# Computing only one token of each mirrored pair directly, and storing the output from compact columns in merged pieces

## The chip, the cores and the metric

The kernel runs on one core of a Trainium2 chip. The metric is the device time of one execution, in microseconds (us). Each kernel was run several times, beside runs of the kernel before on the same chip.

## The reference

The input x has 8 batches of 3008 tokens of 256 elements. The reference takes the real part of a two-dimensional Fourier transform of each batch and feeds every token through a gated feed-forward layer:

```python
X = np.fft.fft(np.fft.fft(x, axis=1), axis=2).real        # 8 x 3008 x 256
t = X.reshape(24064, 256)
out = (np.maximum(t @ w_gate, 0) * (t @ w_val)) @ w_out   # 256 -> 1536 -> 256, float32
```

The input is real, so token r and token 3008 − r of a batch have the same cosine part and sine parts of opposite sign. The kernel uses this: it computes the gate and the value of a "direct" token with two matmuls each, gets the gate of its "mirrored" token with one more matmul, and the mirrored value in most steps on VectorE. A mirrored token is therefore the cheaper one.

## The kernel before

A batch is 3008 = 94 × 32 tokens. The kernel takes it in three blocks of 512 direct columns, each in 12 steps (`f`, one per 128 hidden units), 288 steps in all. The 512 columns are four groups `g` of four quarters of 32. 1536 direct and 1472 mirrored columns make up the 3008 tokens, and each row is stored once. But for 31 pairs both tokens are among the direct ones, although one of them could be had by mirroring.

```python
def mirrored(t):                      # columns whose mirrored token is computed too
    blk = steps[t][1]
    return slice(NB if blk == 0 else 0, 512 - NB if blk == NBLK - 1 else 512)      # NB = 32

def gate(t):                          # value(t, part) has the same form, with wc[1], ws[1]
    ...
    nc.tensor.matmul(e["G"][:], lhsT=wc[0][:, fs], rhs=pq[:, 0, :], start=True, stop=False)
    nc.tensor.matmul(e["G"][:], lhsT=ws[0][:, fs], rhs=pq[:, 1, :], start=False, stop=True)
    nc.scalar.activation(e["gs"][:], e["G"][:], ACTF.Relu)
    # [cut: memset of the 32 columns of h that have no mirrored token]

def out_piece(t, half):               # output matmuls: 128 tokens x 256, summed over 12 f
    ...                               # into po, copied to os (128 x 4 x 256), then:
            if s == 3:
                store(b, blk, sg, os_)

def store(b, blk, sg, os_):           # four transfers of 32 partitions, up to 4 KB a partition
    for u in range(4):
        ka = NKA * u + 4 * blk
        src = os_[32 * u:32 * u + 32].rearrange("p g d -> p (g d)")
        if sg == 0:
            nc.sync.dma_start(out=view(out, (b * S + ka) * D, [[NA * D, NB], [1, 4 * D]]), in_=src)
            continue
        # [cut: the mirrored side, the same with 3 or 4 groups]
```

The next batches are prepared while one is computed. Of the following work the DMAs (all but a small indexed load of POOL's) go through the same queue, SP's, as the stores:

```python
# per batch: load x of batch b+2, fold it on POOL, transform batch b+1 (stage1),
# pass it through DRAM (shuffle_out, shuffle_in), rotate (one matmul), stage2
#     load step, fold step, stage1 steps, shuffle step, rotate step, stage2 steps
plan = {0: (18, 24, (18, 19, 20, 21, 22, 23, 24, 25), 26, 32, (33, 34, 35, 37, 39, 41)),
        1: (7, 13, range(6, 14), 14, 22, (23, 25, 27, 29, 31, 33)),
        2: (7, 13, range(4, 20, 2), 20, 26, (27, 28, 30, 32, 34, 36))}      # batches 2 to 7
op = ctx.enter_context(tc.tile_pool(name="op", bufs=2, space=SB))           # the os tiles
ep = ctx.enter_context(tc.tile_pool(name="ep", bufs=4, space=SB))           # gm, E
```

## Time and profile before

| | before |
|---|---|
| device time, median of 3 runs | 650.03 us (649.75 to 650.68) |
| span of the profiled run | 648.3 us |
| mean granted TensorE clock | 0.987 |

From the page of the kernel before: the span, busy time of each engine (share, instructions), the granted clock in 40 slices in tenths, all DMA packets, the chain that ended last by engine, and the stores.

```profile
span 648.3 us, 12804 instructions
PE 626.1 (97%) x4170; PEld 408.8 (63%) x4246; DVE 565.0 (87%) x889; ACT 425.1 (66%) x813; POOL 508.1 (78%) x716
PEclk9699999999999999999999999999999999999999
DMA packets 32823, 70.77 MB, mean 109 GB/s; under 512 B 4650, under 2 KB 22146, under 8 KB 30754
PE 89%; DVE 6%; issue 2%; DMA 2%; ACT 1%; SPq 0%; DVEq 0%; ACTq 0%
out_dram<-os SPq DMA_DIRECT2D x173, 128.0 KB
```

TensorE bounds this kernel: it is busy 97% of the span and is 89% of the chain. The clock is at 90% or more from the third slice on. A window of one whole batch says the same. Its columns are start:end and length, then busy time and instructions of PE, PEld, DVE, ACT and POOL, the granted clock, the DMA share and GB/s.

```profile
390.00:464.00 74.00, 73.37 (x506) 49.27 (x515) 68.17 (x107) 51.03 (x98) 64.88 (x94) 1.00 0.45 113
```

The timeline of PE around the rotate matmul of the same batch (start, duration, line, what; a bracket at the end would tell idle time before it) has no gap. The rotate, L194, starts 0.22 us after a 512-column matmul.

```profile
390.68 0.38 PE L497 MATMUL V<-pq,ws 128*128 128x512 bf16 x1
390.90 0.18 PE L194 MATMUL psr<-t,rot 128*128 128x12 bf16 x1
390.93 0.60 PE L546 MATMUL po<-wo,h 128*128 128x256 bf16 x4
```

The list of waits (engine, line, what it waited for: total us, times, longest) has nothing at the rotate, and only small entries for what feeds PE. (POOL waits for x in two halves, `xl` and `xh`; the list has 9.3 us more for `xh`.)

```profile
ACT gm L488 <- POOL h L511: 3.4, 6, 0.6
PE G L485 <- ACT gs L475: 2.2, 2, 1.1
POOL eo L99 <- DMA xl<-in_x_dram: 2.2, 1, 2.2
PE po L546 <- DVE os L551: 1.1, 2, 0.6
```

### The profile page before, as it was taken

Reading aid. Unit: us, or ns where it says so; the run is one execution under the profiler, and the core shown is the slowest. Engines: PE = TensorE matmul, PEld = TensorE weight load, DVE = VectorE, ACT = ScalarE, POOL = GpSimd, SP = SyncE. Lnnn points to the kernel's source line nnn. Section 1 sums busy time; section 2 is a strip of 40 time slices with the busy share of each in tenths; the row PEclk is TensorE's granted clock in tenths of the full one; section 3 lists DMA queues with packets and bytes.
Section 4 is the critical chain, followed back from the end, with each engine's and each line's share of the span. In section 5 each row is a group of like instructions: output and inputs, shape, how many; then the busy total and the mean of one; then the engine's idle time right before and its main releaser. Section 6 shows DMA issues by size and latency. Waiting matters only on the chain.

```text
span 648.3 us, 12804 instructions
## 1 busy us (share of the span) xinstructions
PE 626.1 (97%) x4170; PEld 408.8 (63%) x4246; DVE 565.0 (87%) x889; ACT 425.1 (66%) x813; POOL 508.1 (78%) x716
## 2 busy tenths in 40 slices
PE   7888999999999999999999999999999999999995
PEld 3424666666666666666666666666666666666664
DVE  8857688889898998989989998989988988989991
ACT  5465676776766667677676666676666766766660
POOL 9648669967998799968998699967998666666660
PEclk9699999999999999999999999999999999999999
DMA  9792483295125551195334752285312142112113
GB/s 234 241 234 46 104 215 85 69 208 168 40 82 120 143 161 45 47 199 146 81 74 115 165 148 55 50 177 152 96 50 73 31 131 73 50 34 64 32 41 88
DMA packets 32823, 70.77 MB, mean 109 GB/s; under 512 B 4650, under 2 KB 22146, under 8 KB 30754
## 3 DMA queue, kind: packets, MB, share of 16 engines
q1 hardware_dynamic: 30228, 58.03, 33.9%
q0 software_dynamic: 2336, 11.80, 8.7%
q8 instruction: 33, 0.54, 0.4%
q14 instruction: 34, 0.28, 0.1%
q10 hardware_dynamic: 192, 0.13, 0.1%
HBM read 39.77 MB, written 30.96 MB: 109 GB/s over the span
## 4 chain that ended last, share of the span: by engine, by line
PE 89%; DVE 6%; issue 2%; DMA 2%; ACT 1%; SPq 0%; DVEq 0%; ACTq 0%
PE po L546 38%; PE V L497 10%; PE G L474 9%; PE G L485 9%; PE V L495 8%; PE G L473 8%; PE ps L164 2%; PE ps L206 2%; DVE E L505 2%; DVE h L499 1%; PE V L523 1%; PE psw L263 1%; DMA xl<-in_x_dram 1%; DVE eo L136 1%; DVE eo L132 1%
## 5 line engine op out<-in xcount | busy, mean ns | idle before, releaser
L511 POOL TENSOR_TENSOR h<-gm,E 128x480 bf16<-128x480 f32 (+1 forms) x251 | 307.7, 1226 | 90.9 <-DVE E L519 63.9
L546 PE MATMUL po<-wo,h 128*128 128x256 bf16 x2304 | 337.1, 272 | 2.8 <-DVE os L551 1.1
L546 PEld LDWEIGHTS <-h 128*128 128x128 bf16 x2304 | 222.7, 98 | 91.1 <-issue 3.4
L488 ACT ACTIVATE gm<-G 128x480 f32<-128x480 f32 (+1 forms) x288 | 167.4, 581 | 126.8 <-PE G L485 118.7
L499 DVE TENSOR_TENSOR h<-gs,V 128x512 bf16<-128x512 f32 x288 | 195.7, 687 | 17.6 <-ACT gm L488 11.5
L505 DVE SCALAR_TENSOR_TENSOR E<-nb,af,V 128x480 f32<-128x480 bf16 (+1 forms) x245 | 177.6, 725 | 23.3 <-PE V L495 12.6
L475 ACT ACTIVATE gs<-G 128x512 f32<-128x512 f32 x288 | 171.8, 597 | 0.8 <-PE G L474 0.8
L519 DVE SCALAR_TENSOR_TENSOR E<-E,V 128x480 f32<-128x480 f32 (+1 forms) x245 | 161.2, 658 | 0.0
L497 PE MATMUL V<-pq,ws 128*128 128x512 bf16 x287 | 108.7, 379 | 2.2 <-DVE E L505 1.7
L485 PE MATMUL G<-pq,wm 128*128 128x480 bf16 (+1 forms) x288 | 106.7, 370 | 2.2 <-ACT gs L475 2.2
L474 PE MATMUL G<-pq,ws 128*128 128x512 bf16 x281 | 106.5, 379 | 2.2 <-DVE pq L211 0.4
L495 PE MATMUL V<-pq,wc 128*128 128x512 bf16 x255 | 96.6, 379 | 0.0
L473 PE MATMUL G<-pq,wc 128*128 128x512 bf16 x253 | 95.9, 379 | 0.1
L555 ACT COPY os<-po 128x512 f32<-128x512 f32 x94 | 55.0, 585 | 60.2 <-PE po L546 60.2
L104 POOL TENSOR_TENSOR eo<-xl 94x254 bf16<-94x254 f32 (+2 forms) x100 | 74.6, 750 | 0.4
L101 POOL TENSOR_TENSOR xl<-xl,xh 94x510 f32<-94x510 f32 (+2 forms) x50 | 65.9, 1319 | 3.9
L497 PEld LDWEIGHTS <-ws 128*128 128x128 bf16 x288 | 28.2, 98 | 33.7
L474 PEld LDWEIGHTS <-ws 128*128 128x128 bf16 x288 | 28.2, 98 | 31.5 <-issue 0.2
L511 DVE TENSOR_TENSOR h<-gm,V 128x480 bf16<-128x480 f32 (+1 forms) x37 | 24.6, 665 | 22.7 <-ACT gm L488 17.1
L174 ACT CAST t<-ps 96x512 bf16<-96x512 f32 x63 | 36.9, 586 | 5.7 <-PE ps L162 5.2
L495 PEld LDWEIGHTS <-wc 128*128 128x128 bf16 x288 | 28.1, 98 | 11.0 <-issue 4.3
L485 PEld LDWEIGHTS <-wm 128*128 128x128 bf16 x288 | 28.2, 98 | 7.6 <-issue 4.1
(108 smaller groups left out, 348.1 us busy)
## 6 DMA issues: line engine op xcount, KB each, us to landing
out_dram<-os SPq DMA_DIRECT2D x173, 128.0 KB
xl<-in_x_dram SPq DMA_DIRECT2D x7, 1360.0 KB
Td<-t SPq DMA_DIRECT2D x7, 768.0 KB
t<-Td SPq DMA_DIRECT2D x7, 768.0 KB
nb<-Nd SPq DMA_DIRECT2D x24, 128.0 KB
xl<-in_x_dram SPq DMA_DIRECT2D x7, 238.0 KB
xl<-in_x_dram SPq DMA_DIRECT2D x4, 384.0 KB
xh<-in_x_dram SPq DMA_DIRECT2D x4, 384.0 KB
```

Source lines behind the costliest of these rows:

```text
L473: nc.tensor.matmul(e["G"][:], lhsT=wc[0][:, fs], rhs=pq[:, 0, :], start=True, stop=False)
L474: nc.tensor.matmul(e["G"][:], lhsT=ws[0][:, fs], rhs=pq[:, 1, :], start=False, stop=True)
L475: nc.scalar.activation(e["gs"][:], e["G"][:], ACTF.Relu)
L485: nc.tensor.matmul(e["G"][:, cols], lhsT=wm[0][:, f * 128:(f + 1) * 128], rhs=pqt[b, blk][:, 1, cols], start=False, stop=True, skip_group_ ...
L488: nc.scalar.activation(e["gm"][:, cols], e["G"][:, cols], ACTF.Relu)
L495: nc.tensor.matmul(e["V"][:], lhsT=wc[1][:, fs], rhs=pq[:, 0, :], start=True, stop=split(t))
L497: nc.tensor.matmul(e["V"][:], lhsT=ws[1][:, fs], rhs=pq[:, 1, :], start=False, stop=True, skip_group_check=split(t))
L499: nc.vector.tensor_tensor(e["h"][:, 0, :], e["gs"][:], e["V"][:], op=ALU.mult)
L505: nc.vector.scalar_tensor_tensor(e["E"][:, cols], nbt[b, blk][:, cols], af[:, f:f + 1], e["V"][:, cols], op0=ALU.mult, op1=ALU.add)
L511: eng.tensor_tensor(free(e["h"][:], 512 + cols.start + NB - 1, [NB, (cols.stop - cols.start) // NB], [-1, NB]), e["gm"][:, cols].rearrange ...
L519: nc.vector.scalar_tensor_tensor(e["E"][:, cols], e["E"][:, cols], 2.0, e["V"][:, cols], op0=ALU.mult, op1=ALU.subtract)
L546: nc.tensor.matmul(po[:, s % 2, :], lhsT=ht[t - f + ff]["h"][:, sg, g * 128:(g + 1) * 128], rhs=wo[:, ff, :], start=(ff == 0), stop=(ff == ...
```

## The change

The change stops computing both tokens of those 31 pairs directly (1505 direct columns per batch and `f` instead of 1536, and 1504 mirrored instead of 1472), drops the memsets, writes the mirrored product reversed as a whole (one flat pattern), and covers the 128 partitions of an output tile with merged transfers where it can. Columns are compact now, so a tile's rows begin in the middle of a quarter: `store` cuts the tile into pieces of equal stride and merges equal pieces.

```diff
+    LO, HI = NB // 2, 512 - NB // 2
     def mirrored(t):
-        return slice(NB if blk == 0 else 0, 512 - NB if blk == NBLK - 1 else 512)
+        return slice(LO if blk == 0 else 0, HI if blk == NBLK - 1 else 512)
+    def direct(t):
+        return slice(LO - 1 if blk == 0 else 0, HI if blk == NBLK - 1 else 512)
 ...  # gate and value on the columns of direct(t); no memset of h
-        eng.tensor_tensor(free(e["h"][:], 512 + cols.start + NB - 1, [NB, ...], [-1, NB]), ...)
+        eng.tensor_tensor(free(e["h"][:], 512 + n - 1, [-1, n]), e["gm"][:, cols], val[:, cols], op=ALU.mult)
 ...  # out_piece: the last group of a tile may have 112 or 113 tokens; its ACT copy is split in two
+            if last:                                  # the very last tile, group by group
+                nc.vector.tensor_copy(os_[0:m, g:g + 1, :], po[0:m, 0:1, :])
+                store(b, blk, sg, os_, g, g + 1, (nc.sync, nc.scalar) if g == 3 else (nc.sync,))
-        for u in range(4): ...                        # four stores of 32 partitions
+        # parts: (partition, partitions np_, group, groups ng, row), then
+        while k < len(parts):
+            w = 1
+            while ...next part has the same shape, at a constant step...: w += 1
+            queues[n % len(queues)].dma_start(
+                out=view(out, ra * D, [[step * D, w], [NA * D, np_], [1, ng * D]]),
+                in_=os_[p:p + w * np_, ga:ga + ng, :].rearrange("p g d -> p (g d)"))
```

Pieces that result: in block 0, 17, 3x32 and 15 partitions (direct), 3x32, 1, 15, 1, 15 (mirrored); in block 1, 15, 17, 3x32; in block 2, 15, 17, 2x32, 16, 16. "3x32" is one transfer from 96 partitions to three stretches of 32 rows.

## The prediction

> **What bounds it now.** TensorE: PE is busy 97% of the span and 89% of the chain that ended last (the page). By the windows view one batch takes 74.0 us, PE busy 73.4; the timeline shows a 512-column matmul every 0.215 us and an output matmul every 0.109 us, back to back, weight loads hidden. In the list of waits PE waits about 12 us in all. DVE (87%) and POOL (78%) have slack.
>
> **What the change saves.** Each of the 96 (batch, f) pairs loses 31 columns in four direct matmuls and gains 32 in the mirrored gate (and in the mirrored value for 37 unsplit steps): about 8,400 columns net, at 0.215 us per 512 3.5 us of PE, all on the critical path. POOL loses 192 memsets of 123 ns and gains about 33 ns on 167 mirrored products; ACT gets 32 more copies: off the path. Weight loads of 112 or 113 columns should cost nothing: pairs with 96 columns already start 113 ns apart.
>
> **What it adds: badly spread stores.** The built program has 294 rows on the SP queue instead of 159: the 32-partition stores become pieces of 17, 3x32, 15, 1 rows. The Trainium skill ("DMA: Bandwidth & Descriptors", "Why a DMA increments its semaphore by 16 and not by 1") says that the number k of DMA engines is the largest up to 16 that divides the slowest dimension of both sides, and that HWDGE uses the lowest-numbered k. This trace agrees where it can: the 14-partition load shows one early increment, then 14 landings; the one-row Nd store an early one, then one. So 32 rows used 16 engines, but 17 rows use 1, and 3x32 against 96 partitions 3. Engine 0 gets about 50 packets of 4 KB per output tile instead of 8. At 159 ns each (the trace's uncontended packets) a tile keeps it busy 8 us of 12.4; landing goes from 2 us to about 10.
>
> **Is that on the path?** Behind those stores, on the same ring, queue the x load and the shuffle through DRAM. Before: shuffle out 4.4 us, in 4.8, landing 4 us before the rotate matmul. Estimate with an x load: engine 0 gets a store (8.3 us), then loads until about 21 us after the start, then two more stores (16 us); the shuffle lands about 9 us late, and in-order PE waits about 5 us at the rotate matmul. Batches 2 to 5: 5 us each; batch 1 4.6, batch 0 2.5, batch 6 under 1: 28 us. Stalls may drop the granted clock: 3 us. The x fold comes 3 us later on POOL, absorbed by four E buffers. The end gets 14 SP issues of 0.43 us instead of 11: +1.5 us.
>
> **Sum.** 650 - 3.5 + 28 + 3 + 1.5 = 679 us; 80% range 650 to 712. Faster by over 2%: 0.03; within 2%: 0.22; slower by over 2%: 0.75.
>
> **What would show it.** PE busy falls about 3 us while the span grows; the waits gain "PE psr (or its weight load) <- DMA of the shuffle" once per batch, 2 to 8 us; 17-row stores show one late increment, 3x32 stores three; PEclk dips. Wrong if 3x32 stores land on 16 engines or within 3 us, or if no PE gap appears at the rotate.
>
> **What would make it wrong.** Stores split over more engines: then about 649 us. An engine slower than 159 ns a packet, or stores also blocking ACT's output copies (two os buffers): over 700.

## More of the kernel before

The waits of the SP queue show how long the second half of the shuffle waits for the first to land in DRAM: 32.5 us in 8 times, about 4 us each.

```profile
SPq L188 <- DMA Td<-t: 32.5, 8, 7.9
```

At the end, DVE copies the last output tile as soon as PE gives it:

```profile
637.44 0.42 DVE L551 COPY os<-po 128x256 f32<-128x256 f32 x1 [5.28 <-PE po L546]
...
642.72 0.42 DVE L551 COPY os<-po 128x256 f32<-128x256 f32 x1 [1.56 <-PE po L546]
```

## The result, and the profile after

| | before | after |
|---|---|---|
| device time, median | 650.16 us | 716.52 us (711.98 to 716.68, 4 runs) |
| span of the profiled run | 648.3 us | 714.8 us |
| mean granted clock | 0.987 | 0.958 |

The times of before in this table are those of the rounds of after. The change made the kernel slower: ratio 1.1003, 95% interval 1.0959 to 1.1047. A ratio here is the mean time of one kernel's runs over that of the kernel before in the same rounds, so it is not quite the ratio of the medians quoted. Executions over 1.5% slower than the fastest of the same kernel are left out of the means. The output is correct. The same lines of the page after:

```profile
span 714.8 us, 12709 instructions
PE 642.7 (90%) x4215; PEld 421.5 (59%) x4246; DVE 565.3 (79%) x889; ACT 428.8 (60%) x844; POOL 503.2 (70%) x525
PEclk8799999999999999999899998999999999999985
DMA packets 31260, 70.76 MB, mean 99 GB/s; under 512 B 3072, under 2 KB 20584, under 8 KB 29192
PE 52%; DMA 30%; DVE 5%; POOL 3%; ACT 3%; issue 2%; SPq 2%; POOLq 0%; DVEq 0%; ACTq 0%
out_dram<-os SPq DMA_DIRECT2D x32, 384.0 KB
out_dram<-os SPq DMA_DIRECT2D x39, 68.0 KB
```

PE has fewer columns to do, yet its busy time rose by 16.6 us: a lower clock makes the same matmuls longer. The DMA moved the same bytes at a lower mean rate; its share of the chain rose from 2% to 30%. The packets under 512 B fell by about 1,600: if each transfer ends with one small packet per DMA engine that it uses, the change should have 1,578 fewer. By the rule for the number of engines that the prediction names, the 203 stores of before use 16 engines each, 3,248 in all, and the 206 of after 1,670. The difference is 1,578, and the two pages differ by just that (4,650 and 3,072).

The timeline of PE after, at the same rotate. It now starts 6.22 us late, and the matmuls after it start 0.41 us apart until 432, when the 0.21 us of before comes back.

```profile
421.29 0.37 PE L503 MATMUL V<-pq,ws 128*128 128x496 bf16 x1
427.89 0.18 PE L194 MATMUL psr<-t,rot 128*128 128x12 bf16 x1 [6.22 <-DMA t<-Td]
427.91 1.02 PE L554 MATMUL po<-wo,h 128*128 128x256 bf16 x4
...
430.40 0.62 PE L483 MATMUL G<-pq,wc 128*128 128x496 bf16 x1
430.81 0.62 PE L484 MATMUL G<-pq,ws 128*128 128x496 bf16 x1
...
433.58 0.37 PE L490 MATMUL G<-pq,wm 128*128 128x496 bf16 x1
433.79 0.37 PE L483 MATMUL G<-pq,wc 128*128 128x496 bf16 x1
```

Windows of the gap and of the stretch behind it (columns as above): PE does 0.78 us of work in 7.00 us, then works at a granted clock of 0.50.

```profile
421.00:428.00 7.00, 0.78 (x6) 0.31 (x4) 1.45 (x3) 1.06 (x2) 6.92 (x8) 0.87 0.46 135
428.00:432.50 4.50, 4.50 (x21) 2.56 (x20) 2.06 (x4) 1.84 (x4) 2.06 (x3) 0.50 0.24 86
```

The Trainium skill, "TensorE: Matmul & The Clock Gate", section "What's actually happening", puts the half-rate clock down to an idle window of about 3.4 us. This trace agrees in part: between the first and the last gate matmul the clock is at half six times, for 3.41 or 6.83 us each, at six of the seven rotate waits. But two of these waits were only 2.75 and 2.35 us long; the seventh, of 1.74 us, left the clock as it was. So here a wait shorter than 3.4 us was enough.

The chain that ended last names what the rotate waited for (start, duration, what). The first half of the shuffle, issued at 406.31, took 16.15 us to land; only then could the second be issued, and PE was released by it.

```profile
406.31 16.15 DMA Td<-t
...
422.51 5.33 DMA t<-Td
427.84 0.04 issue
427.89 0.18 PE psr L194
```

The SP queue's waits show this for all eight shuffles together (32.5 us before):

```profile
SPq L188 <- DMA Td<-t: 92.3, 8, 15.9
```

And the list of waits, with the entries that were small before and the new ones:

```profile
ACT gm L493 <- POOL h L518: 28.2, 40, 1.8
POOL eo L99 <- DMA xl<-in_x_dram: 32.0, 6, 5.6
PE psr L194 <- DMA t<-Td: 30.0, 7, 6.8
PE G L490 <- ACT gs L485: 8.9, 15, 1.1
PE po L554 <- DVE os L559: 4.3, 1, 4.3
DVE os L559 <- DMA out_dram<-os: 10.4, 1, 10.4
```

At the end, DVE cannot fill the last output tile until an older store has released it, and after its last copy the stores need 14.7 us more, where they needed 5.2 before:

```profile
694.21 0.75 DVE L559 COPY os<-po 128x256 f32<-128x256 f32 x2 [10.35 <-DMA out_dram<-os]
...
699.69 0.42 DVE L559 COPY os<-po 112x256 f32<-112x256 f32 x1 [1.82 <-PE po L554]
```

**Which DMA engines a store uses.** The semaphore of a DMA counts to 16, and the trace has the time of each increment. Counted from the issue:

```
us from issue            first increments   last increments
before  32x1024          1.67, 1.74, ...    ... 1.91, 1.94, 3.44             (16 landings)
after   17 x 1024        0.41 at once       5.24                             (1 landing)
after   3x32 x 1024      1.17 at once       9.15, 9.80, 11.29                (3 landings)
before  shuffle, out     3.66, ...          ... 4.17, 4.26, 4.42
after   shuffle, out     3.40, ...          ... 5.09, 7.34, 8.57, 16.15
```

The 17-partition store has 68 KB and lands at 5.2 us here; the 32-partition store has 128 KB, and all but its last increment are there at about 2 us. Over all of their kind the median of the last increment is 8.9 us (17 partitions, 39 stores), 9.9 us (3x32, 32 stores) and 2.2 us (32 partitions in before, 162 stores). In the shuffle of after, 13 of its 16 engines were done by 5.1 us; three came late, and three come late in each of the seven such shuffles. The trace's packets carry no engine number; that the three are engines 2, 1 and 0, which the stores use, is inferred. This is what the prediction took from the Trainium skill ("DMA: Bandwidth & Descriptors", "Why a DMA increments its semaphore by 16 and not by 1"): 17 rows on one engine, 3x32 on three, 15 on 15. The landings of this trace agree with the number of engines in each of these shapes, and so does the count of small packets above; which engines they are, the trace does not tell. The output tile then puts about 48 packets of 4 KB on engine 0 on average (17 + 32 of the two large pieces, 35 in one kind of tile), where four stores of 32 put 8. A 4 KB packet takes 159 ns in the trace of after, so a tile keeps engine 0 busy for 7.6 us of the 12.3 us between tiles (estimate from these numbers). That is no overload in the mean, but whatever shares the engine can be delayed.

**Where the 66.5 us of span went.** The first gate matmul of each step was compared between the two traces:

```
us longer than in before  batch 0     1     2      3      4     5     6      7   sum | end
after                         2.2   8.0   6.7   11.4   11.0   9.0   3.8   -0.4  51.7 | 14.8
```

"End" is from the last step's gate to the end of the span. To "gain" means, here and below, to take longer than before. Batch 7 has no shuffle and no x load, and it alone is shorter, by the fewer columns. In the other batches the step of the rotate and the one after it gained 41.7 us; PE's wait at the rotate is 30.0 of that, and the rest is about 12 us. The clock is at half for 22.8 us after these waits ended, which costs about half of that, 11.4 us (estimate from the clock's record). The remaining 10 us of the 51.7 (13 once the columns saved, 3 us, are added back) sit in steps 15 to 24, at most about 1 us each, at the time when POOL folds x.

### The profile page after: what moved, and what is told of

Its sections match the earlier page's. It is cut to its first block, busy times and chain, and to the rows that moved or that the text cites. A ratio compares the mean times of both kernels' runs of the same rounds, so it can differ in the third digit from the quotient of the medians.

```text
span 714.8 us, 12709 instructions
## 1 busy us (share of the span) xinstructions
PE 642.7 (90%) x4215; PEld 421.5 (59%) x4246; DVE 565.3 (79%) x889; ACT 428.8 (60%) x844; POOL 503.2 (70%) x525
## 2 busy tenths in 40 slices
DMA packets 31260, 70.76 MB, mean 99 GB/s; under 512 B 3072, under 2 KB 20584, under 8 KB 29192
## 4 chain that ended last, share of the span: by engine, by line
PE 52%; DMA 30%; DVE 5%; POOL 3%; ACT 3%; issue 2%; SPq 2%; POOLq 0%; DVEq 0%; ACTq 0%
PE po L554 22%; DMA xl<-in_x_dram 12%; DMA Td<-t 8%; PE V L503 5%; PE V L501 5%; DMA t<-Td 5%; PE G L484 5%; PE G L490 5%; PE G L483 5%; DMA out_dram<-os 4%; POOL h L518 2%; PE ps L206 2%; SPq L606 1%; PE psw L263 1%; DVE E L511 1%
## 5 line engine op out<-in xcount | busy, mean ns | idle before, releaser
L518 POOL TENSOR_TENSOR h<-gm,E 128x496 bf16<-128x496 f32 (+1 forms) x251 | 312.8, 1247 | 125.5 <-DVE E L524 93.3
L554 PE MATMUL po<-wo,h 128*128 128x256 bf16 (+2 forms) x2304 | 344.5, 277 | 4.8 <-DVE os L559 4.3
L554 PEld LDWEIGHTS <-h 128*128 128x128 bf16 (+2 forms) x2304 | 234.2, 105 | 123.4 <-issue 41.1
L493 ACT ACTIVATE gm<-G 128x496 f32<-128x496 f32 (+1 forms) x288 | 170.2, 591 | 139.4 <-PE G L490 101.9
L505 DVE TENSOR_TENSOR h<-gs,V 128x496 bf16<-128x496 f32 (+2 forms) x288 | 192.9, 677 | 27.5 <-PE V L503 11.7
L511 DVE SCALAR_TENSOR_TENSOR E<-nb,af,V 128x496 f32<-128x496 bf16 (+1 forms) x245 | 180.2, 736 | 32.5 <-PE V L501 26.6
L485 ACT ACTIVATE gs<-G 128x496 f32<-128x496 f32 (+2 forms) x288 | 169.3, 588 | 1.7 <-PE G L484 1.7
L524 DVE SCALAR_TENSOR_TENSOR E<-E,V 128x496 f32<-128x496 f32 (+1 forms) x245 | 163.9, 669 | 0.0
L490 PE MATMUL G<-pq,wm 128*128 128x496 bf16 (+1 forms) x288 | 109.4, 380 | 9.0 <-ACT gs L485 8.9
L484 PE MATMUL G<-pq,ws 128*128 128x496 bf16 (+2 forms) x288 | 109.4, 380 | 1.5 <-DVE pq L211 0.4
L99 POOL TENSOR_TENSOR eo<-xl,xh 94x4 bf16<-94x4 f32 (+2 forms) x50 | 10.8, 216 | 44.4 <-DMA xl<-in_x_dram 32.0
```

The source lines that it names most:

```text
L484: nc.tensor.matmul(e["G"][:, ds], lhsT=ws[0][:, fs], rhs=pq[:, 1, ds], start=False, stop=True)
L485: nc.scalar.activation(e["gs"][:, ds], e["G"][:, ds], ACTF.Relu)
L490: nc.tensor.matmul(e["G"][:, cols], lhsT=wm[0][:, f * 128:(f + 1) * 128], rhs=pqt[b, blk][:, 1, cols], start=False, stop=True, skip_group_ ...
L493: nc.scalar.activation(e["gm"][:, cols], e["G"][:, cols], ACTF.Relu)
L505: nc.vector.tensor_tensor(e["h"][:, 0, 0:ds.stop - ds.start], e["gs"][:, ds], e["V"][:, ds], op=ALU.mult)
L511: nc.vector.scalar_tensor_tensor(e["E"][:, cols], nbt[b, blk][:, cols], af[:, f:f + 1], e["V"][:, cols], op0=ALU.mult, op1=ALU.add)
```

## The experiments

My theory: engine 0 (and 1, 2) is overloaded in bursts by the 17-row and 3x32 stores, and the DMAs on the same queue that PE, POOL and the os tiles wait for become late. Rivals: (a) the compact columns, the 112-column weight loads or the flat reversal cost time themselves; (b) SP has more to issue; (c) only one of the two bad shapes matters.

**spread: everything of the change, but no store on few engines**

```diff
+            # w > 1 groups: w stores of 32 rows; 17 rows: a store of 16 and one of 1
-            queues[n % len(queues)].dma_start(... one transfer of w x np_ partitions ...)
+            for pp, nn, rr in full: queues[n % len(queues)].dma_start(... nn partitions ...)
```

> The kernel after, with each 3x32 or 2x32 store issued as single 32-row stores and each 17-row store as 16 rows and 1 row, nothing else touched; more issues than after (about 345 rows on the SP queue against 294), but about 9 packets of 4 KB for DMA engine 0 per output tile instead of about 48. Theory (stores that use few DMA engines pile up on engine 0): the loss is gone and the saving in columns shows, 645 to 649 us. Rival 1 (the number of store issues, or the eight shared DMA semaphores, is what costs): slower than after, over 716 us. Rival 2 (the new column layout costs: odd widths, split ACT copies, reversed writes): stays over 690 us.

Measured: 655.75 us (654.46 to 656.64, 5 runs), ratio 1.0081 (1.0066 to 1.0096), 7 us above the range expected, though SP issues more transfers than in after. (The trace has 432 DMA instructions on SP, 307 in after and 302 in before; the "rows" of the recorded texts, 159, 294 and 345, match none of these.) The rotate waits are gone. Batches gain −1.1 to 1.2 us against before; the end gains 6.2, as the last tile alone now has 24 issues on the SP queue at about 0.42 us and 3 on ACT's. One line of the list of waits is left over 10 us among the DMA ones:

```profile
POOL eo L99 <- DMA xl<-in_x_dram: 14.5, 5, 3.9
```

So rival (a) falls. Rival (b) cannot explain after, which has only 5 more issues on SP than before; it holds for the end of spread. Nearly all of the loss is in the form of the stores.

**before_bad: the kernel before, with stores cut and merged as in the change**

```diff
-        for u in range(4): ... one store of 32 partitions ...
+        # direct: 17, 15, 3x32 partitions; mirrored: 17 + 15 for the first two or three quarters, else 32
```

The merged 3x32 on the mirrored side would need a negative step in DRAM and is left out. By the pieces engine 0 gets 40 to 56 packets a tile, about 50 on average, as many as in the change; engines 1 and 2 get fewer.

> The kernel before, all its compute unchanged, but its 32-row stores regrouped to imitate the spreading of after: 17 + 15 + 3x32 rows for a direct tile, 17 + 15 rows for two or three of the four quarters of a mirrored tile (40 to 56 packets of 4 KB on engine 0 per tile); the last tile's small stores as before. Theory: 705 to 725 us, with waits of the rotate matmul for the shuffle of 3 to 8 us in most batches. Rival 1: a few us at most, since there are only some 30 more issues. Rival 2: 650 us, since the compute is the old one.

Measured: 689.4 us (686.16 to 691.29), ratio 1.0586 (1.056 to 1.0612). That is less than the 705 to 725 expected: 39 us of loss, not 66. But the computation is that of before, only the stores differ, and the same wait appears at the rotate:

```profile
PE psr L194 <- DMA t<-Td: 18.8, 7, 3.6
```

**only17 and only3x32: one of the two bad shapes taken out**

```diff
 # only17: 17 rows go out as 16 + 1; 3x32 and 2x32 stay merged
+            if np_ == 17: ... 16 + 1 ...
 # only3x32: the merged stores are split into 32 + 32 + 32; 17 rows stay in one
+            if w > 1: ... w stores of 32 ...
```

> The kernel after with only the 17-row stores split into 16 and 1; the 3x32 stores stay on 3 engines: about 36 packets on engine 0 per tile instead of 48, 5.7 us of 12.4. Theory, by the queue worked out for the prediction with these counts: the backlog is gone about 4 us before the shuffle needs it, so the rotate waits nearly vanish (under 1 us each), the tail keeps a few us: 650 to 665 us. If the loss were simply proportional to the packets on engine 0, it would be 716 - 70 * 12/39 = 694 us.

> The kernel after with only the 3x32 and 2x32 stores split into 32-row stores; 17-row stores stay on one engine: about 22 packets on engine 0 per tile, 3.5 us of 12.4. Theory: no backlog left at the shuffle, no rotate wait over 0.5 us, tail within 2 us of before: 646 to 652 us. In proportion to packets it would be 716 - 70 * 26/39 = 669 us.

Measured: only17 677.61 us (672.5 to 681.43), ratio 1.0413 (1.0362 to 1.0465); only3x32 665.1 us (664.6 to 666.62), ratio 1.0226 (1.0211 to 1.0242). Both are above what was expected. By the pieces, engine 0 gets about 36 packets a tile in only17, 21 in only3x32, 9 in spread and 48 in after; among these four the times follow that order: 677.6, 665.1, 655.8, 716.5. (before_bad does not fit in: about 50 packets and 689.4 us. So the packets on engine 0 are not the whole measure; what else counts was not tested.) Rival (c) falls: both shapes matter. The misses taught more. In only3x32 no rotate wait is listed, and yet batches 2 to 5 gain 12.6 us. Two waits that grew there are

```profile
ACT gm L493 <- POOL h L518: 22.2, 28, 2.8
POOL eo L99 <- DMA xl<-in_x_dram: 24.5, 5, 6.7
```

That is a second route, as the waits read: x lands late, POOL waits at the fold, so its products h behind it come late, their gm and E buffers stay taken, ACT waits for a gm buffer, and PE for ACT (9.2 us in this kernel, 2.2 before). The prediction had called this absorbed.

**tail_fix: change only batch 7's stores and the last tile**

```diff
-                store(..., g, g + 1, (nc.sync, nc.scalar) if g == 3 else (nc.sync,))
+                store(..., g, g + 1, (nc.sync, nc.scalar))
+            if b == B - 1 and blk > 0 and g1 - g0 == 4 and (w > 1 or np_ == 17): ... as spread ...
```

> The kernel after, changed only for the last two blocks of the last batch: their full tiles are stored in 32-, 16-, 15- and 1-row pieces, and the last tile's small stores go alternately to the two store queues, unsplit. If the 14.8 us that after loses behind its last gate matmul come from stores that hold the two output buffers (and a little from store issues in a row): 716 - 14 = 700 to 705 us, and the stretch from the last gate to the end is 20 to 22 us instead of 35. If that stretch were long for another reason (the matmuls with 112 columns, the copies): over 712 us.

Measured: 697.45 us (693.47 to 700.87), ratio 1.0725 (1.0672 to 1.0777). The end takes 24.6 us, 10.6 less than in after but more than the 20 to 22 expected, and DVE no longer waits for a store. About 10 us more came off in batches 0 to 6, which the edit does not touch (and 1.8 us were lost before the first gate): the rotate waits are 23.2 us here, 30.0 in after. These waits are not a constant from run to run, and differences of that size between the slow kernels are not read below.

**early_shuffle: shuffle of batches 3 to 7 eight steps earlier**

```diff
-            2: (7, 13, range(4, 20, 2), 20, 26, (27, 28, 30, 32, 34, 36))}
+            2: (7, 13, range(4, 12), 12, 26, (27, 28, 30, 32, 34, 36))}
```

> The kernel after with the stage-1 work and the shuffle of batches 3 to 7 moved 8 steps (16 us) earlier, the rotate matmul left where it is; the stores are not touched. If the rotate waits (five of them, 25 us, and about 8 us of half clock after them) are only the shuffle coming late: those waits are under 0.5 us each and the time falls to 680 to 690 us. If engine 0 is simply too busy to get its work done: the waits turn up elsewhere, over 705 us.

Measured: 689.47 us (689.18 to 690.45), ratio 1.0608 (1.059 to 1.0626), as expected. With bad stores unchanged, the rotate waits are left only in batches 0 and 1, whose shuffles were not moved:

```profile
PE psr L194 <- DMA t<-Td: 5.3, 2, 3.5
```

SP still waits 86.4 us for the first halves of the shuffles (92.3 in after): they land as late as ever, only earlier than needed. Batches 2 to 5 still gain 3.2 to 4.9 us each; POOL's wait for x (26.5 us) is still there, and ACT's for os tiles is 7.3 us. This shows that the wait at the rotate is latency of the shuffle, which slack in the schedule can hide. The five batches moved take 25.4 us less than in after, half clock included.

**early_load and load_act: x three steps earlier, or x through another queue**

```diff
 # early_load
-            1: (7, 13, ...),  2: (7, 13, ...)
+            1: (4, 13, ...),  2: (4, 13, ...)
 # load_act
-            at(t0 + tl, load_x, b + 2, nc.sync)
+            at(t0 + tl, load_x, b + 2, nc.scalar)
```

> The kernel after with the load of x issued at step 4 instead of 7 in batches 1 to 5, so before the store that it queued behind. If the slow steps 15 to 24 of batches 2 to 5 (about 2 us each) are POOL starting its fold late on x: the wait of POOL's fold for x falls from 32 to under 10 us, those steps are as before, and the time falls by 6 to 12 us to 704 to 711 us; the rotate waits stay, since engine 0 has as much to do. If POOL's lateness is absorbed, as the prediction said: 716 us.

> The kernel after with the loads of x (all but the first two) issued from the ACT queue, on a ring of their own, instead of behind the stores on the SP ring; stores untouched. The early_load run took POOL's wait for x away but put the store behind the load, which then held the output buffers and cost as much. [...]If the slow steps 15 to 24 of batches 2 to 5 come from x reaching POOL late: POOL's wait for xl falls from 32 to under 12 us, these steps are as before, and the time falls to 700 to 710 us, rotate waits staying (20 us or more). If not: 714 to 720 us.

Measured: early_load 718.31 us (715.64 to 722.63), ratio 1.1059 (1.101 to 1.1109); load_act 723.77 us (721.53 to 725.56), ratio 1.1133 (1.1107 to 1.1158). Both missed: nothing was gained. In early_load POOL waits 4.7 us for this load, not 32.0 (and 11.7 us, once, for its other half), but a wait of ACT that was 3.3 us in after has grown:

```profile
ACT os L566 <- DMA out_dram<-os: 33.4, 5, 12.0
```

In load_act the same line has 38.6 us. The x load now falls together with the stores that have to free an os tile, of which there are two; ACT waits for one, and PE, which waits for ACT, stands still for 4 to 11 us at step 15. Delay taken from one user of engine 0 reappeared at another. That a queue of its own did not help x (it still waits 22.2 us) agrees with the Trainium skill, "DMA: Bandwidth & Descriptors", "Issuing engines are not separate DMA queues", which says that DMAs of all issuing engines run on the same 16 engines and interleave.

**os4: the change with four os tiles instead of two**

```diff
-    op = ctx.enter_context(tc.tile_pool(name="op", bufs=2, space=SB))
+    op = ctx.enter_context(tc.tile_pool(name="op", bufs=4, space=SB))
```

> The kernel after with four output buffers instead of two, nothing else. The wait of the last tile's copies for a buffer (10.4 us) goes, but the stores behind it must still drain through engine 0: the stretch after the last gate falls from 35 to 27 to 31 us. Rotate waits stay (25 to 32 us). 707 to 714 us. If the buffers were the main cause in the batches too: under 695 us.

Measured: 709.3 us (702.82 to 711.67), ratio 1.0886 (1.0823 to 1.0949). The total is in the range expected, the end is not: 33.0 us, hardly less than the 35.2 of after. The wait of DVE for a tile is gone, but in the last 24 us SP waits 10.4 us, in 4 times, for older stores to land before it can issue the rest. More buffers alone do not cure it.

**hidden and hidden_os4: bad stores kept, every known wait given slack**

```diff
 # hidden = early_shuffle + load_act, batch 7 spread as in tail_fix, the last tile stored whole on two queues
+                if g == 3:
+                    store(b, blk, sg, os_, 0, 4, (nc.sync, nc.scalar))
 # hidden_os4 = hidden with bufs=4 for the os tiles
```

> All stores of after as they are but for the last two blocks of the last batch (spread, and the last tile stored whole), with the shuffle 8 steps earlier and the x loads on the ACT queue: the badly spread stores remain, only what waited for them is moved. If the loss is the sum of rotate waits with their half clock (about 40 us), x late on POOL (about 13) and the tail (about 15): what remains are the rotate waits of batches 0 and 1, 655 to 668 us. If engine 0's load costs in itself: over 680 us.

> The hidden run (badly spread stores kept, shuffle earlier, x on its own ring, good tail) lost 6 to 8 us at step 15 of each batch instead, where ACT waited for a store to free one of the two output buffers. Here there are four output buffers, nothing else changed. If engine 0 is full only in bursts and each loss is whichever consumer has the least slack: the step-15 stall goes, no wait over 2 us takes its place, and the time is 652 to 668 us although engine 0 moves the same packets. If engine 0 is full altogether: over 680 us, with the stall at another step.

Measured: hidden 695.36 us (692.62 to 697.45), ratio 1.069 (1.0662 to 1.0719), far above what was expected. The rotate wait is 0.3 us and the end 20.0, but the os tiles took over:

```profile
ACT os L567 <- DMA out_dram<-os: 39.3, 6, 7.1
PE psr L194 <- DMA t<-Td: 0.3, 1, 0.3
```

hidden_os4 took 674.88 us (672.13 to 677.04), ratio 1.0367 (1.0335 to 1.0398), still 7 us above its range. The stall at step 15 is gone, and the end is 20.1. What is left is in batches 0 and 1 (7.6 and 8.7 us), whose shuffles were not moved, and 2 to 4 us in each of batches 2 to 5. One of the three waits below, of 2.5 us, is in batch 4, whose shuffle was moved:

```profile
PE psr L194 <- DMA t<-Td: 15.3, 3, 7.7
```

Outside batch 7, engine 0 carries the same packets as in after; yet batches 2 to 6, which gained 41.9 us there, gain 10.8 here, by buffers, schedule and the queue of x alone. So engine 0 is short only in bursts: what the stores cost is latency at each place that has no slack, one after the other, not bandwidth over the whole run.

**best: spread for whole tiles, x load earlier in batches 1 to 7, last tile on both queues**

```diff
+            if g1 - g0 == 4 and (w > 1 or np_ == 17): ... as spread ...
-                store(..., (nc.sync, nc.scalar) if g == 3 else (nc.sync,))
+                store(..., (nc.sync, nc.scalar))
 # and 4 instead of 7 as the load step in both later plans
```

> The columns of after with full tiles stored in 32-, 16-, 15- and 1-row pieces, the last tile's stores unsplit on both queues, and the load of x at step 4. If the 9 us that the spread kernel lacks of the forecast are store issues in its tail (6 us) and x arriving behind eight issues (3 us): 644 to 648 us, faster than before by the 3.5 us of columns. If the new layout costs something of its own: 650 us or more.

Measured: 658.76 us (657.93 to 659.82, 4 runs), ratio 1.0131 (1.0113 to 1.0149): a miss, and slower than spread. Batch 1 alone gains 6.6 us at step 15, where ACT waits 6.1 us for an os tile and POOL 11.0 for the other half of x: in that batch step 4 is the wrong place for the load. The end is 24.9 us, with the group-wise last tile still in merged stores.

**best2, and before_early as its control**

```diff
 # best2: spread everywhere, last tile stored once as a whole on two queues, load step 4 only in plan 2
+                if g == 3:
+                    store(b, blk, sg, os_, 0, 4, (nc.sync, nc.scalar))
 # before_early: the kernel before, with load step 4 in plan 2
-            2: (7, 13, range(4, 20, 2), 20, 26, ...
+            2: (4, 13, range(4, 20, 2), 20, 26, ...
```

> The columns of after, all tiles stored in 32-, 16-, 15- and 1-row pieces, the last tile stored whole on both queues, the x load at step 4 in batches 2 to 5 but still at 7 in batch 1 (where the best run lost 7 us at step 15, as POOL was not ready for x). Each batch from 2 on should be 0.36 to 0.39 us shorter than before, batch 1 about 1 us, the tail within 1.5 us of before's 20.4: 646 to 650 us. If the new columns cost something of their own: 651 us or more.

> The kernel before with the x load at step 4 instead of 7 in batches 2 to 5, as in best2: a control, to tell what of best2's time is the moved load. POOL waits for x 11 us in before, but PE is hardly held by it: 648 to 650 us.

Measured: best2 646.46 us (645.8 to 647.09, 5 runs), where the kernel before had 650.35 in the same rounds: ratio 0.994 (0.9927 to 0.9954). It is 0.6% faster than the kernel before: clear of the noise. The control, before_early, is at 650.87 us (649.04 to 651.94), ratio 1.0014 (1.0 to 1.0028), so the earlier load is not what the kernel before lacked. From the page of best2:

```profile
span 644.8 us, 12844 instructions
PE 623.1 (97%) x4215; PEld 414.6 (64%) x4246; DVE 563.9 (87%) x889; ACT 426.8 (66%) x844; POOL 503.2 (78%) x525
```

Batches 2 to 7 are each 0.36 to 0.39 us shorter than in before, and the end 0.8 us. This is what the change was for, with nothing in its way.

## Why the prediction was right or wrong

The direction was right, and so was the main mechanism. The size was not: 679 predicted, 716.5 measured, just above the upper end of the range, 712.

- **Columns, "3.5 us of PE": right.** Batch 7 of after and batches 2 to 7 of best2 are 0.36 to 0.39 us shorter, about 3 us for eight batches.
- **Weight loads and the flat reversal "should cost nothing": right**, as best2 shows.
- **Store shapes, 17 rows on one engine and 3x32 on three: right**, by the landings and the count of small packets; before_bad shows that the shapes alone cost tens of us. The 294 store rows "instead of 159" are not in the traces: 307 DMA instructions on SP, 302 before.
- **Rotate, "28 us": right.** The trace has 30.0 us in 7 waits, 1.7 to 6.8 us each; early_shuffle takes the later five away. The sum fits better than its parts, which is luck: batch 2 has 2.75 us where 5 were forecast, batch 3 has 6.8, and batch 6 has 2.35 where under 1 was.
- **"Stalls may drop the granted clock: 3 us": mechanism right, size wrong.** The rotate's step and the one after it gained 41.7 us, of which 30.0 is the wait: about 12 us. After six of the seven waits PE worked at half clock for another 2.7 to 5.1 us. I had seen the waits coming and counted their aftermath at a quarter of its size. This term failed in its size.
- **"The x fold comes 3 us later on POOL, absorbed by four E buffers": this step failed.** POOL waited up to 5.6 us at one x load, in 6 batches, and the lateness went on over gm buffers and ACT to PE: about 13 us. That figure is the remainder of a subtraction; of the waits themselves, ACT's for POOL's products grew from 3.4 to 28.2 us and PE's for ACT from 2.2 to 8.9. That the route exists is seen in only3x32 (no rotate wait, 12.6 us lost in batches 2 to 5) and in best2, in which POOL waits 1.5 us for this load and the loss is gone (for the other half it waits 13.7 us there, 9.3 in before, without loss).
- **"The end gets 14 SP issues of 0.43 us instead of 11: +1.5 us": this step failed.** The end grew by 14.8 us: the last copy comes 5.3 us later after the last gate, behind DVE's wait for an os tile, and the stores after it drain 9.5 us longer. From 694.66 on SP issues 17 small stores (not 14), waits 8.7 us between them, in 4 times, for older stores to land, and issues the last one at 710.70. I counted the issuing of the last stores and not the landings that both the copies and the issues wait for, although the same text had engine 0 at 8 us a tile. tail_fix took 10.6 us of it away. The danger to the two os buffers was named under "what would make it wrong", for ACT, and was not in the sum.

Sum: 650 − 3 + 30 + 12 + 13 + 14.8 = 716.8. (It has to come out near the measured time, as the 12 and the 13 are remainders; the clock's record gives 11.4 for the 12.) The misses are 9 (clock), 13 (POOL) and 13.3 (end), of 37.5 in all; the rotate and the columns account for the other 2, about.

What stays open: how much of the 13 us in steps 15 to 24 belongs to which half of x; no experiment held the clock at full rate during the waits, so the 12 us is read from the trace and not from a run without it; why before_bad, with as many packets on engine 0, loses 27 us less than the change; and how much of each delay is SP itself waiting for older stores to land before it can issue (29.1 us in 12 times over the whole of after).

## What to carry to other kernels

Before merging or recutting a store, work out how many DMA engines each piece gets: here one of 17 partitions (68 KB), and one of 3x32 (384 KB), landed later than the stores of 32 partitions (128 KB), and DMAs behind them landed late too. When a resource is congested in bursts, don't price only the first consumer that waits: list each wait that has no slack (the shuffle, the input, the output buffers, the end), for a fix of one can hand the delay to the next. And price the end of the kernel by the landing of its last stores, not by their issue.

## What the Trainium skill lacked or had wrong

- "DMA: Bandwidth & Descriptors", section "Rules for kernel authors", advises one 128-partition transfer in place of two transfers to disjoint partition halves. Another row of the same table ("Use all 16 engines") asks for an outermost dimension that is a multiple of 16, but the first row does not point to it. Here merging three stores of 32 partitions into one transfer with 3 as its outermost dimension took it from 16 engines to 3: landings at 9.15, 9.80 and 11.29 us where a store of 32 needs about 2. With only3x32, which undoes the merge and leaves the 17-row stores, the time falls from 716.5 to 665.1 us.
- The same page, "Why a DMA increments its semaphore by 16 and not by 1", gives the rule for the number of engines but not what a small number costs those behind it. Runs here: 68 KB on one engine landed at 5.2 us at one of the quiet places and at 8.9 us in the median; a shuffle of 16 engines behind such stores landed at 16.15 us, not 4.4, and its completion came from three late engines.
- "TensorE: Matmul & The Clock Gate", section "What's actually happening", gives about 3.4 us of idleness for the fall to half clock. In the trace of after, waits of 2.75 and 2.35 us were followed by half clock as well, and one of 1.74 us was not.
- The same page, "Weight-path perf modes — Fast Weight Load (FWL) and DoubleRow", ties fast weight loads to 128 weights. The trace agrees: in best2 a weight load of 112 columns of the output matmuls took 130 ns and one of 128 columns 98 ns. No loss shows there: batches 2 to 7 were each 0.36 to 0.39 us shorter than before.
